# A spectrum stage interleaved with the next one, a half-group inverse over two PSUM buffers, and one DMA in place of four: a long convolution with gate and MLP on one core

## The chip, the cores and the metric

The kernel runs on one core of a Trainium2 chip. The metric is the device time of one execution in microseconds (us), as a median over several executions. Executions of one kernel agree within about 2%. Times from the profile ("span") are 1.7 to 2.2 us shorter than the device times.

In the views, PE, DVE, ACT, POOL and SP stand for TensorE, VectorE, ScalarE, GpSimd and SyncE, and PEld for TensorE's weight loads. An eviction is a copy out of PSUM, the memory into which matmuls write; a bank is here a piece of it of 128 x 512 f32, as in the views of evictions.

## The reference

```python
x  = A_q                                         # 2048 tokens x 512 channels
h  = x + A(_layernorm(x), k, v, shift_k, ssm_k, ssm_D)
h2 = h + relu(_layernorm(h) @ w1) @ w2           # 512 -> 1376 -> 512

def A(q, k, v, shift_k, ssm_k, ssm_D):
    kv = causal_4_tap(k, shift_k) * v
    y  = irfft(rfft(kv padded to 4096) * rfft(ssm_k padded to 4096))[:2048]
    return q * (y + kv * ssm_D)
```

The Fourier transforms are done as matmuls: 4096 = 64 x 64, so each transform is a "stage 1" and a "stage 2" with tables of sines between.

## The kernel before

The order on TensorE is: transposes and stage 1 of ssm_k (with the four taps of kv between), transposes of kv, spectrum of ssm_k (stage 2), stage 1 of kv, stage 2 of kv with the product, inverse stage 1, then groups of four token tiles through inverse stage 2, gate, layernorm and MLP. In the views, pst are the transposes, ps a stage 1, ps2k the spectrum of ssm_k, u and psy the product, psi and pz the two inverse stages, zt an evicted pz, st the statistics of a layernorm, pt and hlnT its transposed rows, ps1m and ps2m the two halves of the MLP. The parts that matter here (cut where dots stand):

```python
def _tokens(src2d, t0, nt):          # four patterns of 32 rows: token = 64 b + 16 a + t
    return [bass.AP(..., offset=... + (16 * a + t0) * D, ap=[[64 * D, 32], [1, nt * D]]) for a in range(4)]
...
def stage1(fl, a_out, engs, between=None):
    for gb in range(8):              # 64 small matmuls into 4 banks, then 4 evictions
        pss = [psum.tile([P, 8, 64], F32, tag="ps", ...) for r in range(4)]
        for gi in range(8):
            for f, first in ((f1hi, True), (f1lo, False)):
                for rg in range(4):  nc.tensor.matmul(out=pss[rg][:, gi, :], ...)
        for rg in range(4):  copy(engs[...], a_out[:, :, j0:j0 + 8], pss[rg]...)
...
for kp in range(16):                 # spectrum of ssm_k: 8 matmuls, an add on VectorE, a cast on ScalarE
    ...
stage1(xfl, a1x, "ADADADAA")         # then stage 1 of kv
...
for a, src in enumerate(_tokens(x_d, 0, NT)):     # x, 2 MB, after the product has freed the space
    nc.sync.dma_start(out=xh[32 * a:32 * a + 32, :, :]..., in_=src)
...
pzp = pl.push("psZ", bufs=1, space=PSUM)          # one buffer of 4 banks for the inverse
...
qln = ln1(0, on_act=True)
inv2_copy(0, inv2(0))
hln = new_rows(0)
gate(0, [0, 1], qln, hln, on_act=True)
gate(0, [2, 3], qln, hln, on_act=True)
pz = inv2(1)
transposes(0, hln)
mlp1(0, slice(0, 2 * P))
transposes(2, hln)
inv2_copy(1, pz)
mlp1(0, slice(2 * P, 4 * P))
chain(1)                             # layernorm, gate, layernorm, DMA transposes of group 1
inv2_copy(2, inv2(2))
mlp2(0)
chain(2)
...
```

## Time and profile before

| | before |
|---|---|
| time, median (3 fast runs) | 240.22 us (240.03 to 240.64) |
| span of the profile | 238.6 us |
| TensorE, VectorE, ScalarE busy | 206.1, 154.2, 130.7 us |

On the page, each digit of a strip is one fortieth of the span, about 6 us; PEclk is the clock that TensorE was granted, in tenths. The clock strip of the kernel before:

```profile
PEclk9999999999955899999999779999999999999998
```

There are two places of lowered clock: stage 1 of kv (65.6 to 79.3 us) and the stretch around the start of the MLP (two pieces of 3.41 us, from 133.9 and from 140.7). Before each of the two places TensorE was idle for a good part of the time: in the 3.41 us before, it was busy for 2.2 and for 1.2 us.

### The profile page before, as it was taken

To read this page: it belongs to the slowest core of one execution; us is meant where nothing else is said; L and a number is where in the kernel's file an instruction comes from. 1 tells how busy PE (TensorE), PEld (TensorE's weight loads), DVE (VectorE), ACT (ScalarE), POOL (GpSimd) and SP (SyncE) were. 2 spreads that over 40 slices of the span, in tenths; PEclk is the share of its full clock that TensorE was granted. 3 is DMA by queue.
4 is the path that set the end of the run, shared out by engine and by line. 5 is a ranking of instruction groups with operands and counts; after the bars stand their busy time and mean duration, and the time that the engine had idled before them with its cause. 6 is when DMAs were issued, how large, how long until landed. Compare 5 with 4: busy or idle time off the path is not lost.

```text
span 238.6 us, 7218 instructions
## 1 busy us (share of the span) xinstructions
PE 206.1 (86%) x3100; PEld 145.8 (61%) x3100; DVE 154.2 (65%) x299; ACT 130.7 (55%) x241; POOL 62.7 (26%) x88
## 2 busy tenths in 40 slices
PE   0486998999767999998989678899999999979992
PEld 0473555999646999978986546764446444434440
DVE  7886986877655989977995882822577257740031
ACT  3779464666775688897992338912262327105500
POOL 6399700000003999975000001020022002200000
PEclk9999999999955899999999779999999999999998
DMA  6999910000000000009992000023200420042011
GB/s 212 286 206 157 190 34 4 3 1 0 3 5 3 3 1 0 3 1 201 195 368 70 3 3 0 3 46 69 61 8 3 93 71 17 0 91 65 23 44 44
DMA packets 30191, 15.45 MB, mean 65 GB/s; under 512 B 25584, under 2 KB 29008, under 8 KB 30032
## 3 DMA queue, kind: packets, MB, share of 16 engines
q1 hardware_dynamic: 29088, 14.93, 28.3%
q8 instruction: 24, 0.39, 0.7%
q10 hardware_dynamic: 1072, 0.07, 0.4%
q14 instruction: 7, 0.06, 0.1%
HBM read 7.08 MB, written 2.10 MB: 38 GB/s over the span
## 4 chain that ended last, share of the span: by engine, by line
PE 79%; ACT 9%; DMA 5%; DVE 4%; issue 2%; SPq 0%; ACTq 0%
PE ps1m L486 16%; PE ps2m L496 15%; PE pz L417 9%; PE psi L389 6%; PE pst L196 5%; PE psy L326 5%; PE pkv L254 5%; PE u L226 4%; PE u L228 4%; DMA sk<-in_A_ssm_k_dram 4%; PE ps L212 3%; PE ps2k L226 3%; PE ps2k L228 3%; ACT zt L425 2%; ACT c2c L174 2%
## 5 line engine op out<-in xcount | busy, mean ns | idle before, releaser
L488 ACT ACTIVATE h1T<-ps1m 128x512 bf16<-128x512 f32 (+3 forms) x55 | 28.0, 515 | 39.3 <-PE ps1m L486 38.5
L486 PE MATMUL ps1m<-hlnT,w 128*128 128x512 bf16 (+3 forms) x220 | 40.5, 346 | 4.5 <-ACT hlnT L508 2.2
L496 PE MATMUL ps2m<-w,h1T 128*128 128x512 bf16 (+1 forms) x176 | 38.7, 379 | 0.0
L486 PEld LDWEIGHTS <-w 128*128 128x128 bf16 (+1 forms) x220 | 22.6, 103 | 22.1 <-issue 5.3
L499 DVE TENSOR_TENSOR o<-ps2m,xh 128x512 bf16<-128x512 f32 x16 | 11.0, 691 | 38.2 <-PE ps2m L496 38.2
L316 DVE TENSOR_TENSOR t<-u,kf 128x704 fp32r<-128x704 f32 x32 | 27.1, 889 | 4.8 <-ACT usb L312 4.8
L496 PEld LDWEIGHTS <-h1T 128*128 128x128 bf16 (+1 forms) x176 | 17.0, 98 | 21.1 <-issue 0.8
L316 POOL TENSOR_TENSOR t<-usb,kf 128x320 fp32r<-128x320 f32 x32 | 28.7, 924 | 3.4 <-ACT usb L312 2.3
L417 PE MATMUL pz<-bp,ecore 32*32 32x128 f32 x1024 | 22.1, 387 | 4.2 <-ACT zt L425 2.2
L434 POOL TENSOR_SCALAR rstd<-mv 128x4 f32<-128x4 f32 x6 | 1.4, 229 | 88.5 <-DVE mv L441 88.5
L417 PEld LDWEIGHTS pz<-bp,ecore 32*32 32x32 f32 x1024 | 15.8, 108 | 9.8 <-issue 2.9
L439 DVE BATCH_NORM_STATS2 st<-xh 128x6 f32<-128x512 bf16 x32 | 19.8, 680 | 0.0
L328 ACT CAST kf<-psy 128x512 fp32r<-128x512 f32 x32 | 18.4, 645 | 1.6
L389 PE MATMUL psi<-dre,kf 128*128 128x256 f32 x64 | 15.8, 288 | 0.9 <-ACT kf L328 0.9
L425 ACT CAST zt<-pz 128x512 bf16<-128x512 f32 x16 | 8.2, 602 | 13.9 <-PE pz L417 13.9
L326 PE MATMUL psy<-t,ipos 128*128 128x512 f32 x48 | 15.8, 390 | 0.0
L389 PE MATMUL psi<-dim,kf 128*128 128x256 f32 x64 | 15.4, 283 | 0.0
L254 PE MATMUL pkv<-kT,wdiag 128*128 128x512 bf16 x64 | 15.2, 381 | 0.0
L196 PE MATMUL pst<-ident,sk 128*128 128x128 bf16 x64 | 6.7, 299 | 9.2 <-DMA sk<-in_A_ssm_k_dram 9.2
L201 ACT CAST a1k<-ps 128x512 fp32r<-128x512 f32 x20 | 10.4, 593 | 6.7 <-PE ps L212 6.7
L283 DVE TENSOR_TENSOR kf<-ps2k,dtab 128x512 fp32r<-128x512 f32 x16 | 11.0, 694 | 3.5 <-PE ps2k L228 3.4
L284 ACT CAST kf<-ps2k 128x512 fp32r<-128x512 f32 x16 | 10.2, 641 | 5.5 <-PE ps2k L228 5.3
(108 smaller groups left out, 410.0 us busy)
## 6 DMA issues: line engine op xcount, KB each, us to landing
sk<-in_A_ssm_k_dram SPq DMA_DIRECT2D x1, 2048.0 KB, 8.4
xh<-in_A_q_dram SPq DMA_DIRECT2D x4, 512.0 KB, 8.6
out_dram<-o SPq DMA_DIRECT2D x64, 32.0 KB, 1.6
w<-in_B_w_dram SPq DMA_DIRECT2D x1, 1376.0 KB, 15.1
w<-in_B_w_dram SPq DMA_DIRECT2D x1, 1280.0 KB, 18.2
hlnT<-hln SPq DMA_TRANSPOSE x12, 2.5
w<-in_B_w_dram SPq DMA_DIRECT2D x1, 96.0 KB, 17.8
dtab<-in_A_ssm_D_dram ACTq DMA_DIRECT2D x2, 32.0 KB, 8.4
```

Source lines behind the costliest of these rows:

```text
L196: nc.tensor.transpose(out=pst[:, i, :], in_=src[:, :, :, 8 * q + i], identity=ident[:])
L226: nc.tensor.matmul(out=ps[:, kk, :], lhsT=w_re[:, k1, :], rhs=a_in[:, k1, :], start=True, stop=False, skip_group_check=True)
L254: nc.tensor.matmul(out=ps[:], lhsT=wdiag[:, rg, j, :], rhs=kT[c][:, rg, 16 - j:CH + 16 - j], start=(j == 0), stop=(j == KS - 1))
L316: eng.tensor_tensor(out=t[:, :, j, :], in0=in0.unsqueeze(1).to_broadcast([P, 2, n, 2]), in1=kfr[:, :, j, ks], op=ALU.mult)
L326: nc.tensor.matmul(out=psy[:], lhsT=m_[:], rhs=t_.rearrange("p j k -> p (j k)"), start=first, stop=not first)
L328: nc.scalar.copy(out=kf[:, s, :, 2 * kp:2 * kp + 2], in_=psy[:].rearrange("p (j k) -> p j k", k=2))
L389: nc.tensor.matmul(out=ps[:, i, :], lhsT=kf[:, c, 4 * m:4 * m + 4, :].rearrange("p r k -> p (r k)"), rhs=d[:].rearrange("p a b -> p (a b)" ...
L417: nc.tensor.matmul(out=pz[32 * a:32 * a + 32, r4, l4, :], lhsT=ecore[rows, rho, n2, :], rhs=rhs, start=(rho == 0), stop=(rho == 1), tile_p ...
L439: nc.vector.bn_stats(out=st[:, t % 4, :], in_=xh[:, t, :])
L486: nc.tensor.matmul(out=ps1[:fsz, :], lhsT=w1[:, c, fc * P:fc * P + fsz], rhs=hlnTs[sc][:, c, part], start=(c == 0), stop=(c == DC - 1))
L488: nc.scalar.activation(out=h1s[sc][:fsz, fc, part], in_=ps1[:fsz, :], func=ACT.Relu)
L496: nc.tensor.matmul(out=ps2[:], lhsT=h1s[sc][:ksz, fc, i * P:(i + 1) * P], rhs=w2[:ksz, fc, :], start=(fc == 0), stop=(fc == NFC - 1))
```

## The change

The change has five parts. (A) Half of the ssm_k spectrum runs alone, the other half between the first four groups of stage 1 of kv; kv's result overwrites the half of ssm_k's that is used up, so columns and tables are laid out by halves. (B) The inverse stage 2 of the first two groups goes in halves over two PSUM buffers of four banks. (C) The layernorm of the next group is issued ahead of mlp2. (D) The four patterns of 32 rows become one pattern of (4, 32) rows, for the load of x and for the output stores. (E) The small table dtab is loaded in four transfers instead of two. Cut to its core:

```diff
-    return [bass.AP(..., offset=src2d.offset + (16 * a + t0) * D, ap=[[64 * D, 32], [1, nt * D]])
-            for a in range(4)]
+    return bass.AP(..., offset=src2d.offset + t0 * D, ap=[[16 * D, 4], [64 * D, 32], [1, nt * D]])
...
-    for kp in range(16):
-        ... spectrum step kp ...
-    stage1(xfl, a1x, "ADADADAA")
+    for kp in range(8):
+        spectrum_k(kp)
+    for gb in range(8):
+        stage1(gb, xfl, lambda h, j: a1x[:, h, :, j:j + 8], "ADADADAA" if gb >= 4 else "ADAD")
+        if gb < 4:
+            spectrum_k(8 + 2 * gb)
+            spectrum_k(9 + 2 * gb)
...
-    for a, src in enumerate(_tokens(x_d, 0, NT)):
-        nc.sync.dma_start(out=xh[32 * a:32 * a + 32, :, :].rearrange("p t d -> p (t d)"), in_=src)
+    nc.sync.dma_start(out=xh[:].rearrange("p t d -> p (t d)"), in_=_tokens(x_d, 0, NT))
...
-            for a, dst in enumerate(_tokens(out_d, t, 1)):
-                nc.sync.dma_start(out=dst, in_=o[32 * a:32 * a + 32, :])
+            nc.sync.dma_start(out=_tokens(out_d, t, 1), in_=o[:])
...
-    inv2_copy(0, inv2(0))
     hln = new_rows(0)
-    gate(0, [0, 1], qln, hln, on_act=True)
-    gate(0, [2, 3], qln, hln, on_act=True)
-    pz = inv2(1)
+    for ts in ([0, 1], [2, 3]):
+        inv2_copy(0, ts)
+        gate(0, ts, qln, hln, on_act=True)
+    for ts in ([0, 1], [2, 3]):
+        inv2_copy(1, ts)
+    pl.pop("psZ0")                   # two buffers of 4 banks until here
+    ... push psT, psM, psZ ...
     transposes(0, hln)
-    mlp1(0, slice(0, 2 * P))
-    transposes(2, hln)
-    inv2_copy(1, pz)
+    mlp1(0, slice(0, 2 * P), lambda: transposes(2, hln))
     mlp1(0, slice(2 * P, 4 * P))
-    chain(1)
-    inv2_copy(2, inv2(2))
+    chain(1, ln1(1))
+    inv2_copy(2)
+    qln = ln1(2)
     mlp2(0)
-    chain(2)
+    chain(2, qln)
...
```

More of the change, by code (lines that the diff above doesn't have):

```diff
@@ L51, in _tokens @@
     D = src2d.shape[1]
-    return [bass.AP(tensor=src2d.tensor, offset=src2d.offset + (16 * a + t0) * D, ap=[[64 * D, 32], [1, nt * D]])
-            for a in range(4)]
+    return bass.AP(tensor=src2d.tensor, offset=src2d.offset + t0 * D, ap=[[16 * D, 4], [64 * D, 32], [1, nt * D]])
 @with_exitstack
@@ L97 @@
     nc.scalar.dma_start(out=wsh[:], in_=A_shift_k.rearrange("(r p) j -> p r j", p=P))
-    dtab = consts.tile([P, DC, 64], BF16, name="dtab")
+    dtab = consts.tile([P, 2, DC, 32], BF16, name="dtab")
     for dp in range(2):
-        src = bass.AP(tensor=A_ssm_D.tensor, offset=A_ssm_D.offset + 64 * dp, ap=[[0, 64], [P, DC], [1, 64]])
-        nc.scalar.dma_start(out=dtab[64 * dp:64 * dp + 64, :, :], in_=src)
+        for h in range(2):
+            src = bass.AP(tensor=A_ssm_D.tensor, offset=A_ssm_D.offset + 64 * dp + 32 * h,
+                          ap=[[0, 64], [P, DC], [1, 32]])
+            nc.scalar.dma_start(out=dtab[64 * dp:64 * dp + 64, h, :, :], in_=src)
     vT = vp.tile([P, DC, S], BF16, name="vT")
@@ L161 @@
     f1f = early.tile([P, 64], F32, name="f1_f")
-    _sin(f1f[:, 0:32], t1[:, 0:32], 128)
-    _sin(f1f[:, 32:64], t1[:, 32:64], 128, neg=True)
+    f1v = f1f[:].rearrange("p (h c k) -> p c h k", h=2, c=2)
+    _sin(f1v[:, 0], t1[:, 0:32].rearrange("p (h k) -> p h k", h=2), 128)
+    _sin(f1v[:, 1], t1[:, 32:64].rearrange("p (h k) -> p h k", h=2), 128, neg=True)
     cc = wp.tile([P, 32, P], F32R, name="c2c")
@@ L203, in copy, with stage1, col @@
             nc.vector.tensor_copy(out=o, in_=i)
-    def stage1(fl, a_out, engs, between=None):
-        for gb in range(8):
-            pss = [psum.tile([P, 8, 64], F32, tag="ps", name=f"ps1_{r}") for r in range(4)]
-            for gi in range(8):
-                for f, first in ((f1hi, True), (f1lo, False)):
-                    for rg in range(4):
-                        rows = slice(32 * rg, 32 * rg + 32)
-                        nc.tensor.matmul(out=pss[rg][:, gi, :],
-                                         lhsT=fl[rows, 8 * gb + gi, :, :].rearrange("p d n -> p (d n)"),
-                                         rhs=f[rows, :], start=first, stop=not first, tile_position=(32 * rg, 0))
-            for rg in range(4):
-                j0 = 64 * rg + 8 * gb
-                copy(engs[(4 * gb + rg) % len(engs)], a_out[:, :, j0:j0 + 8], pss[rg][:].rearrange("p g c -> p c g"))
-            if between is not None:
-                between(gb)
+    def stage1(gb, fl, a_out, engs):
+        pss = [psum.tile([P, 8, 64], F32, tag="ps", name=f"ps1_{r}") for r in range(4)]
+        for gi in range(8):
+            for f, first in ((f1hi, True), (f1lo, False)):
+                for rg in range(4):
+                    rows = slice(32 * rg, 32 * rg + 32)
+                    nc.tensor.matmul(out=pss[rg][:, gi, :],
+                                     lhsT=fl[rows, 8 * gb + gi, :, :].rearrange("p d n -> p (d n)"),
+                                     rhs=f[rows, :], start=first, stop=not first, tile_position=(32 * rg, 0))
+        for rg in range(4):
+            copy(engs[(4 * gb + rg) % len(engs)], a_out(gb // 4, 32 * rg + 8 * (gb % 4)),
+                 pss[rg][:].rearrange("p g c -> p c g"))
+    def col(k1, c):
+        return 32 * (k1 // 16) + 16 * c + k1 % 16
     def stage2(ps, a_in, kp, s):
@@ L225, in stage2 @@
             w_re, w_im = ((cc, cs), (cn, cc))[s]
-            nc.tensor.matmul(out=ps[:, kk, :], lhsT=w_re[:, k1, :], rhs=a_in[:, k1, :], start=True, stop=False,
+            nc.tensor.matmul(out=ps[:, kk, :], lhsT=w_re[:, k1, :], rhs=a_in(col(k1, 0)), start=True, stop=False,
                              skip_group_check=True)
-            nc.tensor.matmul(out=ps[:, kk, :], lhsT=w_im[:, k1, :], rhs=a_in[:, 32 + k1, :], start=False, stop=True,
+            nc.tensor.matmul(out=ps[:, kk, :], lhsT=w_im[:, k1, :], rhs=a_in(col(k1, 1)), start=False, stop=True,
                              skip_group_check=True)
@@ L246 @@
     nc.gpsimd.memset(dim[:].bitcast(F32), 0.0)
-    a1k = slotA.tile([P, 64, 256], F32R, tag="A", name="a1k")
+    a1 = slotA.tile([P, 64 * 256], F32R, tag="A", name="a1")
+    a1k = a1[:].rearrange("p (c j) -> p c j", j=256)
+    a1x = a1[:].rearrange("p (h c j) -> p h c j", h=2, j=P)
     def taps(u):
@@ L261, in two_taps @@
         taps(2 * gb + 1)
-    stage1(kfl, a1k, "ADAADADA", two_taps)
+    for gb in range(8):
+        stage1(gb, kfl, lambda h, j: a1k[:, :, P * h + j:P * h + j + 8], "ADAADADA")
+        two_taps(gb)
     for pq in halves:
@@ L276, with spectrum_k @@
     kf = slotB.tile([P, 2, 256, 32], F32R, tag="B", name="kf")
-    dcol = dtab[:].rearrange("p r g -> p (r g)").unsqueeze(2).to_broadcast([P, 256, 2])
-    for kp in range(16):
+    dcol = dtab[:].rearrange("p h r g -> p (h r g)").unsqueeze(2).to_broadcast([P, 256, 2])
+    def spectrum_k(kp):
         ks = slice(2 * kp, 2 * kp + 2)
@@ L281 @@
         for s in range(2):
-            stage2(ps[s], a1k, kp, s)
+            stage2(ps[s], lambda c: a1k[:, c, :], kp, s)
         nc.vector.tensor_tensor(out=kf[:, 0, :, ks], in0=ps[0][:].rearrange("p k j -> p j k"), in1=dcol, op=ALU.add)
         nc.scalar.copy(out=kf[:, 1, :, ks], in_=ps[1][:].rearrange("p k j -> p j k"))
-    a1x = slotA.tile([P, 64, 256], F32R, tag="A", name="a1x")
-    stage1(xfl, a1x, "ADADADAA")
+    for kp in range(8):
+        spectrum_k(kp)
+    for gb in range(8):
+        stage1(gb, xfl, lambda h, j: a1x[:, h, :, j:j + 8], "ADADADAA" if gb >= 4 else "ADAD")
+        if gb < 4:
+            spectrum_k(8 + 2 * gb)
+            spectrum_k(9 + 2 * gb)
     pl.pop("psF")
@@ L308, in product @@
             u = psum.tile([P, 2, 256], F32, tag=f"u{s}", name=f"u{s}")
-            stage2(u, a1x, kp, s)
+            stage2(u, lambda c: a1x[:, :, c, :], kp, s)
             usb = prod.tile([P, 256 - NJ, 2], F32, tag=f"usb{s}", name=f"usb{s}", bufs=2)
@@ L385 @@
         ps = psum.tile([P, 2, 2 * P], F32, tag="ps", name="psi1")
+        h, r, g = b // 16, b // 4 % 4, b % 4
+        m0 = 16 * r + 8 * h + 2 * g
         for i in range(2):
@@ L390 @@
                                  rhs=d[:].rearrange("p a b -> p (a b)"), start=(c == 0), stop=(c == 1))
-        copy("ADAADADA"[b % 8], bp[:, 2 * b:2 * b + 2, :, :, :].rearrange("p g a b c -> p g (a b c)"), ps[:])
+        copy("ADAADADA"[b % 8], bp[:, m0:m0 + 2, :, :, :].rearrange("p g a b c -> p g (a b c)"), ps[:])
         if b in (3, 10, 17):
@@ L398 @@
     pl.pop("psI")
-    pzp = pl.push("psZ", bufs=1, space=PSUM)
-    ptp = pl.push("psT", bufs=1, space=PSUM)
-    psum = pl.push("psM", bufs=3, space=PSUM)
+    pzp = pl.push("psZ0", bufs=2, space=PSUM)
     ep = pl.push("ep", bufs=2)
@@ L406, with inv2 @@
     zts, hlnTs, h1s = {}, {}, {}
-    def inv2(q):
+    def inv2(q, l4s=(0, 1, 2, 3)):
         pz = pzp.tile([P, 4, 4, P], F32, tag="pz", name="pz")
-        for l4 in range(4):
+        for l4 in l4s:
             for rho in range(2):
@@ L420, in inv2, with inv2_copy @@
         return pz
-    def inv2_copy(q, pz):
-        zts[q] = hp.tile([P, 4, D], BF16, tag="zt", name="zt")
-        for l4 in range(4):
+    def inv2_copy(q, l4s=(0, 1, 2, 3)):
+        pz = inv2(q, l4s)
+        if q not in zts:
+            zts[q] = hp.tile([P, 4, D], BF16, tag="zt", name="zt")
+        for l4 in l4s:
             nc.scalar.copy(out=zts[q][:, l4, :].rearrange("p (m r) -> p m r", r=4),
@@ L469, in new_rows, with chain @@
         return ep.tile([P, 4, D], BF16, tag="hln", name="hln")
-    def chain(q):
-        qln = ln1(q)
+    def chain(q, qln):
         hln = new_rows(q)
@@ L476, in chain, with mlp1 @@
             nc.sync.dma_start_transpose(out=hlnTs[q][:, :, i * P:(i + 1) * P], in_=hln[:, i, :])
-    def mlp1(sc, part=slice(0, 512)):
+    def mlp1(sc, part=slice(0, 512), midway=None):
         if sc not in h1s:
@@ L482, in mlp1 @@
         for fc in range(NFC):
+            if fc == NFC // 2 and midway is not None:
+                midway()
             fsz = min(P, DFF - fc * P)
@@ L510 @@
     qln = ln1(0, on_act=True)
-    inv2_copy(0, inv2(0))
     hln = new_rows(0)
-    gate(0, [0, 1], qln, hln, on_act=True)
-    gate(0, [2, 3], qln, hln, on_act=True)
-    pz = inv2(1)
+    for ts in ([0, 1], [2, 3]):
[4 more added lines that the diff above has]
+    pl.pop("psZ0")
+    ptp = pl.push("psT", bufs=1, space=PSUM)
+    psum = pl.push("psM", bufs=3, space=PSUM)
+    pzp = pl.push("psZ", bufs=1, space=PSUM)
     transposes(0, hln)
-    mlp1(0, slice(0, 2 * P))
-    transposes(2, hln)
-    inv2_copy(1, pz)
+    mlp1(0, slice(0, 2 * P), lambda: transposes(2, hln))
     mlp1(0, slice(2 * P, 4 * P))
-    chain(1)
-    inv2_copy(2, inv2(2))
+    chain(1, ln1(1))
+    inv2_copy(2)
+    qln = ln1(2)
     mlp2(0)
-    chain(2)
+    chain(2, qln)
     mlp1(1)
-    inv2_copy(3, inv2(3))
+    inv2_copy(3)
+    qln = ln1(3)
     mlp2(1)
-    chain(3)
+    chain(3, qln)
     for sc in (2, 3):
```

## The prediction

The sum came to 240.2 - 4.9 + 2.0 - 1.5 + 0.1 = 235.9 us with four engines for x, and to 229.8 with 16; the forecast between them was 235.0.

> **What bounds the kernel now.** I read the page's table of busy time first. TensorE is busy 206.1 of 238.6 us, but VectorE (154.2) and ScalarE (130.7) take turns in setting the pace, so an average says little. I then cut the span into stages by busy time of each engine in each stretch. Columns: stretch, its length, then busy us (and instructions) of PE, weight loads, DVE, ACT, POOL, then granted clock, DMA share, GB/s.
>
> ```profile
> core 0: us, PE busy (x) PEld busy (x) DVE busy (x) ACT busy (x) POOL busy (x), PEclk, DMA share, GB/s
> ...
> 45.60:61.10 15.50, 15.50 (x138) 15.37 (x140) 11.90 (x17) 10.09 (x16) 0.00 (x0) 1.00 0.01 2
> 61.10:74.80 13.70, 8.36 (x514) 6.67 (x513) 7.82 (x13) 10.77 (x21) 0.79 (x2) 0.67 0.02 5
> ```
>
> The first row is the ssm_k spectrum: TensorE is full, both evicting engines have a third free. The second is stage 1 of kv: 512 tiny matmuls, which TensorE could do in about 5 us (0.61 us for each of 8 groups), but 32 evictions of PSUM pace it and TensorE even drops to 0.67 clock. The timeline gives the cost of evictions:
>
> ```profile
> 46.89 2.00 DVE L283 TENSOR_TENSOR kf<-ps2k,dtab 128x512 fp32r<-128x512 f32 x3
> ...
> 61.83 2.54 ACT L201 CAST a1x<-ps 128x512 fp32r<-128x512 f32 x5
> 65.04 2.54 ACT L201 CAST a1x<-ps 128x512 fp32r<-128x512 f32 x5 [0.66 <-PE ps L212]
> ```
>
> So 0.51 us for an ACT eviction, 0.67 for a DVE spectrum add. After this, the product stage (to 105 us) is DVE's, and untouched. Then the chain of waits, for the inverse stage 2 (L417) and what follows:
>
> ```profile
> 131.31 2.06 ACT zt L425 x4
> 133.37 0.04 issue
> 133.42 4.58 PE pz L417 x188
> ...
> 140.02 1.02 ACT hlnT L508
> ...
> 148.00 1.01 ACT hlnT L508
> 149.01 1.96 ACT zt L425 x4
> ...
> 212.29 2.45 DMA hlnT<-hln
> ```
>
> TensorE stands still for 2.2 us while ACT empties the only pz buffer, 1.1 us twice for hlnT, 0.8 us because zt delays the ReLUs, and 1.5 us for the last DMA transpose. From 155 us TensorE is otherwise back to back. The last lines I need concern x, which the first layernorm reads:
>
> ```profile
> 107.25 1.74 SPq L344 DMA_DIRECT2D xh<-in_A_q_dram  x4
> ...
> xh<-in_A_q_dram SPq DMA_DIRECT2D x4, 512.0 KB, 8.6
> ...
> 124.19 2.46 DVE L439 BATCH_NORM_STATS2 st<-xh 128x6 f32<-128x512 bf16 x4
> ```
>
> x is issued at 107.25 and used at 124.19; DVE comes to it straight from the last bp copy, so the load has slack. Its slowest quarter lands 11.5 us after issue, near 119: some 5 us of slack.
>
> [...]
>
> **The change, part by part.** Times are on the clock of the profile of before.
>
> *A, spectrum beside stage 1.* The first 8 of 16 spectrum steps run alone: 8 x 0.96 = 7.7 us, to 53.3. Then four rounds of one stage-1 group and two spectrum steps. TensorE: 0.61 + 2 x 0.96 = 2.53 us. DVE: 2 x 0.63 + 2 x 0.67 = 2.59. ACT: 2 x 0.51 + 2 casts of 0.64 at most = 2.3. The round is even, 2.6 us, so four end at about 64.0 (first evictions at 54.05, TensorE's last work of them at 63.4, a little lag on DVE). The other four groups stand alone as before: in the trace two pairs of groups take 5.75 us from the first eviction (61.83) to the tenth ACT copy (65.04 + 2.54). End 64.0 + 5.8 = 69.8 against 74.7 now: -4.9 us, all on the path. The second half's eviction overwrites what the last spectrum step has read by then, so no new wait. I count nothing for the clock, which can still drop in the lone half.
>
> *B, half groups over two buffers, x on time.* ACT's order becomes root, zt half, root, zt half, ... Let X be the start of the x statistics. From the trace: statistics to normalised rows 4.8 us; gate of a half 4.3, its root after 3.0. Gate one X+4.8 to X+9.1; root ends X+8.1; zt of rows 2,3 to X+9.2; gate two ends X+13.4, its root X+12.4; zt of group 1's first half X+13.4 frees the banks for the transposes; its second half X+14.4; hlnT copy X+15.4; the MLP starts at X+15.5. With X = 124.2 that is 139.7 instead of 141.1. Then mlp1(0): 6.4 us in the half-clock start, 0.5 for the transposes now inside it, 5.1 for the second half without waits: it ends 12.2 us later, at 151.9 instead of 155.0: -3.0.
>
> *C, norms ahead of mlp2.* The last transposes come several us earlier (a 5.5 us norm leaves the path before gate 3): the 1.5 us wait at 213 goes. -1.5.
>
> *D, one DMA for four.* [...] 4 engines would carry 2 MB, 512 KB each. Estimate of one engine's rate: the DMA view of 100 to 130 us, in slices of 0.75 us, peaks at 407 GB/s over 16 while w1 and w2 load, 25.4 GB/s each:
>
> ```profile
> GB/s 0 0 0 0 0 0 0 11 0 0 66 284 284 131 240 218 153 306 131 240 262 131 284 58 183 283 385 407 385 355 352 354 347 348 302 71 48 0 0 0
> ```
>
> 524,288 B / 25.4 = 20.6 us; plus 1 us to the first byte, x lands near 129.2, and X moves from 124.2 to 129.2, +5.0 us, exposed in full because B's whole chain hangs on X. B then gives -3.0 + 5.0 = +2.0. The outputs, too, go over 4 engines: 32 rows of 1 KB each; at 48 ns a row (packet time in the trace) 1.5 us instead of 0.1. Three issues fewer (3 x 0.42 us) at the very end pay for it: +0.1. Over 16 engines it would be -1.0.
>
> *E.* dtab in 4 small transfers: 1.8 us more of issue on ACT, which idles 2.1 us there. 0.
>
> Sum with D [...]: 240.2 - 4.9 + 2.0 - 1.5 + 0.1 = 235.9. With 16 engines: 240.2 - 4.9 - 3.0 - 1.5 - 1.0 = 229.8.
>
> **Rivals.** R1: x is late (sum 235.9). For it: [...] that X leads the whole chain. Against: [...] the lowering might reorder the pattern. R2: x is in time (229.8). I give R1 three in four. R3: A gains less: the lone stage-1 groups wait for instructions (1 us issue gaps inside pairs in the chain), or interleaving makes DVE fall behind and hold banks; all 8 are used in a round. That would leave -3 of -4.9 and make R1 238. R4: TensorE, starved while x is awaited, sits at half clock longer into mlp1(0): +1 to +1.5 on R1, to 237. R5: eight small evictions more evenly spread keep the clock at 1.0 into the product: a further -0.4.
>
> **Range and chances.** The two sums are 6 apart. Weighted 3:1 they give 234.4; I take 235.0, near the likelier one. Range 229.5 to 238.0: R2 with a small bonus below, R1 with R3 above. The 2% line is 235.4. R2 lies below it nearly surely (0.24 of 0.25); of R1, its middle being 235.9 and its spread 1.5, about 0.4 lies below (0.30 of 0.75). That is 0.54; slower by 2% needs A to fail as well: 0.03.
>
> **What would show it.** A: the stretch from the last pst transposes to the first u takes 24.2 us, not 29.1. B: no ACT wait between the first two inverse groups other than on buffer two; no hlnT wait in mid mlp1(0). C: no DMA wait before the last mlp1. D decides: DVE's first wait on x. If the statistics wait on the x load for about 5 us, and its landing time is near 21 us, R1 holds; if x lands in under 16 us, R2. I am wrong altogether if A's stretch hardly shrinks or a new wait opens in the MLP.

The 1 us to the first byte is that of the kernel before: x is issued at 107.25 us and its first row starts at 108.24.

## The result

The changed kernel is slower: 260.06 us median (257.51 to 261.73, 4 runs) beside 240.43 us for the kernel before (4 runs, one of them, 243.92, slow). The ratio is 1.079 (95% interval 1.068 to 1.089). A ratio here is the mean time of one kernel's runs over that of the other's of the same rounds, so it is not quite the ratio of the medians. Executions over 1.5% slower than the fastest of the same kernel are left out of the means. The outputs are correct. The prediction said 235.0 us, range 229.5 to 238.0: wrong by 25 us, and on the wrong side.

The one profile of the changed kernel is of a run 1.6% above that kernel's fastest. Nothing below rests on that 1.6%, which is 4.2 us: the main wait is 24.6 us, and a wait of 23.3 us for the same load is found in a fast run (run 3).

The clock strip and the statistics row of the changed kernel's page show at once where to look. In the row: busy us, mean ns of one, then idle time before them and what ended it. Before:

```profile
L439 DVE BATCH_NORM_STATS2 st<-xh 128x6 f32<-128x512 bf16 x32 | 19.8, 680 | 0.0
```

Changed:

```profile
PEclk9997999999959999999965555599999999999998
...
L455 DVE BATCH_NORM_STATS2 st<-xh 128x6 f32<-128x512 bf16 x32 | 19.8, 679 | 24.6 <-DMA xh<-in_A_q_dram 24.6
```

VectorE stood still for 24.6 us for x, and TensorE ran at half clock from 131.6 to 169.2 us. The chain of waits of the changed kernel (start, length, what):

```profile
105.53 41.60 DMA xh<-in_A_q_dram
147.16 2.47 DVE st L455 x4
...
159.08 1.94 ACT zt L441 x4
161.07 1.02 PE pt L523 x8
162.17 1.02 ACT hlnT L524
163.23 4.42 PE ps1m L503 x20
```

The load of x takes 41.6 us from issue to landing, and the MLP cannot start before 163.2. Next, both kernels cut into the same six stretches: from the last transposes of kv to the first matmul of the product, to the first inverse matmul of stage 2, to the MLP's first matmul, to the inverse of group 2, to the last matmul, to the end. The first, the third and the fourth line carry the reading (columns as in the prediction). Before:

```profile
45.71:74.73 29.02, 23.68 (x640) 21.86 (x639) 19.71 (x29) 20.75 (x37) 0.79 (x2) 0.84 0.01 3
...
124.99:141.08 16.09, 12.16 (x520) 8.80 (x521) 11.80 (x36) 5.20 (x9) 0.00 (x0) 0.88 0.11 33
141.08:154.97 13.89, 12.01 (x107) 9.93 (x114) 8.48 (x23) 10.72 (x26) 1.28 (x2) 0.89 0.00 1
```

Changed:

```profile
47.84:73.43 25.59, 22.18 (x641) 20.69 (x639) 20.33 (x31) 20.21 (x35) 0.79 (x2) 0.94 0.01 4
...
123.28:163.23 39.95, 12.37 (x520) 9.25 (x521) 14.28 (x43) 7.00 (x13) 0.35 (x2) 0.60 0.21 56
163.23:176.33 13.10, 13.10 (x107) 10.69 (x114) 10.65 (x32) 8.95 (x22) 2.20 (x3) 0.77 0.07 13
```

The whole account, with the lengths of the other stretches:

| stretch | before | changed | difference |
|---|---|---|---|
| start to the end of kv's transposes | 45.71 | 47.84 | +2.1 |
| spectrum and stage 1 of kv | 29.02 | 25.59 | -3.4 |
| product, inverse stage 1 | 50.26 | 49.85 | -0.4 |
| inverse stage 2 to the MLP's start | 16.09 | 39.95 | +23.9 |
| first mlp1 | 13.89 | 13.10 | -0.8 |
| to the last matmul | 79.08 | 77.80 | -1.3 |
| to the end | 4.55 | 5.47 | +0.9 |
| span | 238.6 | 259.6 | +21.0 |

So the stretches of A and C and the first mlp1 are shorter, in sign as forecast, and one stretch eats it all.

### The profile page after: what moved, and what is told of

The parts are those of the page before. It is cut to its first block, busy times and chain, and to the rows that moved or that the text cites. A ratio compares the mean times of both kernels' runs of the same rounds, so it can differ in the third digit from the quotient of the medians.

```text
span 259.6 us, 7149 instructions
## 1 busy us (share of the span) xinstructions
PE 205.9 (79%) x3085; PEld 146.0 (56%) x3100; DVE 154.4 (59%) x301; ACT 130.2 (50%) x239; POOL 62.2 (24%) x88
## 4 chain that ended last, share of the span: by engine, by line
PE 66%; DMA 19%; DVE 6%; ACT 5%; issue 2%; POOLq 0%; DVEq 0%; ACTq 0%
DMA xh<-in_A_q_dram 16%; PE ps1m L503 16%; PE ps2m L513 15%; PE psy L341 6%; PE pst L198 5%; PE pkv L261 5%; PE pz L431 4%; DMA sk<-in_A_ssm_k_dram 3%; PE u L229 3%; PE ps2k L229 3%; PE u L231 3%; PE ps L214 3%; PE ps2k L231 3%; DVE st L455 2%; ACT c2c L176 2%
## 5 line engine op out<-in xcount | busy, mean ns | idle before, releaser
L503 PE MATMUL ps1m<-hlnT,w 128*128 128x512 bf16 (+3 forms) x217 | 41.3, 352 | 1.3 <-ACT hlnT L524 1.2
L455 DVE BATCH_NORM_STATS2 st<-xh 128x6 f32<-128x512 bf16 x32 | 19.8, 679 | 24.6 <-DMA xh<-in_A_q_dram 24.6
L203 ACT CAST a<-ps 128x512 fp32r<-128x512 f32 x38 | 19.9, 594 | 9.4 <-PE ps L214 9.2
L205 DVE CAST a<-ps 128x512 fp32r<-128x512 f32 x26 | 16.8, 686 | 5.8 <-PE ps L214 5.7
L447 ACT ACTIVATE rstd<-mv,eps_t 128x2 f32<-128x2 f32 (+1 forms) x3 | 0.9, 297 | 31.8 <-DVE mv L457 31.8
L261 PE MATMUL pkv<-kT,wdiag 128*128 128x512 bf16 x56 | 15.9, 402 | 0.6 <-issue 0.2
```

The source lines that it names most:

```text
L203: nc.scalar.copy(out=o, in_=i)
L261: nc.tensor.matmul(out=ps[:], lhsT=wdiag[:, rg, j, :], rhs=kT[c][:, rg, 16 - j:CH + 16 - j], start=(j == 0), stop=(j == KS - 1))
L455: nc.vector.bn_stats(out=st[:, t % 4, :], in_=xh[:, t, :])
L503: nc.tensor.matmul(out=ps1[:fsz, :], lhsT=w1[:, c, fc * P:fc * P + fsz], rhs=hlnTs[sc][:, c, part], start=(c == 0), stop=(c == DC - 1))
```

## The experiments

The theory after reading the traces: D alone makes the loss; the x load runs on four engines (in the trace 116 of its 128 rows of 16 KB start with four under way; in the kernel before it is 16 to 18 for 111 of 128), and those slow one another down. The rivals: the interleaving or the half-group order is itself harmful; or the engines do not slow one another down.

**1. The changed kernel with x in four transfers again.**

```diff
-    nc.sync.dma_start(out=xh[:].rearrange("p t d -> p (t d)"), in_=_tokens(x_d, 0, NT))
+    for a, src in enumerate(_tokens4(x_d, 0, NT)):
+        nc.sync.dma_start(out=xh[32 * a:32 * a + 32, :, :].rearrange("p t d -> p (t d)"), in_=src)
```

> The changed kernel with one thing undone: x is loaded in four transfers of 32 rows again (outputs still in one transfer each). Theory D (the x load on four engines, [...] is nearly the whole loss): x lands 11 to 12 us after its issue, before VectorE is free for the statistics, no DMA wait there; time 234 to 237 us, against 240.2 before and about 260 changed. Rival I (the interleaved stage or the half-group inverse is itself the loss): the time stays at 245 us or above though x lands in time.

Measured 236.78 us (235.67 to 237.44), ratio to before 0.985 (0.978 to 0.991). One statement is worth 23 us. The statistics no longer wait for x. The interleaving and the half groups are not the loss.

**2. The same with the output stores in four as well.**

> The changed kernel with both the x load and the output stores in four transfers again. Theory D: as the run with only the x load undone, less 0.5 to 1 us at the end, because the last store lands sooner [...] (233 to 236 us). Rival (one store per tile is cheaper, three issues of 0.42 us saved): this run is up to 1 us slower than the run with only the x load undone.

Measured 235.92 us (234.13 to 236.38), ratio 0.980 (0.974 to 0.987). That is 0.9 us under the first run, as the theory said, though the intervals overlap. This kernel has everything of the change but D, so the stretches of A, B and C are best read from it. From the same cuts as above, those of the spectrum with stage 1 of kv, of the first mlp1, and of the rest to the last matmul (its stretch from the first inverse matmul to the MLP, 16.02 us, is in the chain further down):

```profile
46.54:71.65 25.11, 21.77 (x641) 20.36 (x639) 20.32 (x31) 20.17 (x35) 0.79 (x2) 0.99 0.02 4
...
137.23:150.22 12.99, 12.99 (x107) 10.76 (x113) 10.77 (x32) 8.85 (x22) 1.81 (x5) 0.78 0.16 21
150.22:227.44 77.22, 76.69 (x813) 37.77 (x820) 29.25 (x71) 24.17 (x42) 4.68 (x7) 1.00 0.21 43
```

**3. The kernel before with x in a single transfer, nothing else.**

> The kernel before with one thing added: x in a single transfer over (4, 32) rows. Theory D: landing about 41 us after issue instead of at most 11.5, VectorE's first statistics wait 24 to 25 us for it, time 263 to 267 us: slower than the changed kernel, which gains a few us elsewhere. Rival I: the load costs only a few us (under 246), the rest of the loss comes from the other parts of the change.

Measured 260.37 us (260.12 to 261.22), ratio 1.084 (1.077 to 1.091). The loss alone, without the rest of the change. I had expected 263 to 267, so this missed by 3 us, and its chain shows why:

```profile
107.26 40.28 DMA xh<-in_A_q_dram
147.56 2.47 DVE st L444 x4
...
160.59 6.63 PE ps1m L491 x44
```

From the statistics to the MLP it takes 13.0 us here, but 16.1 us in the changed kernel (147.16 to 163.23). When x is late, the old order runs all of group 1's inverse (152.6 to 158.9) while VectorE works on the gates. In the new one the last evictions of the inverse stand in ScalarE's queue behind the root of the second gate (158.79), and the transposes follow them at 161.07. B costs about 3 us in that state, by one profile of each. So the late x explains all of the loss, and B a part of what A and C could have given back.

**4. The kernel before with each output tile in one store.**

> The kernel before with one thing added: each output tile in one transfer over (4, 32) rows. Theory: 32 rows of 1 KB go one after another on each of four engines; the tail after the last output add grows from 3.8 to about 4.7 us, time 241.0 us (+0.3 to +1.2). Rival (issue cost rules): three issues fewer at the end, 239.2 us (-1).

Measured 240.85 us, ratio 1.002 (0.996 to 1.008): too small to tell in the time. In the profile the end after the last matmul is 5.0 us (233.62 to 238.6) against 4.55. The three saved issues do not pay for the four engines, but by little (in the changed kernel's trace, which has the same stores, the 128 rows of the last one take 1.76 us, mostly in fours that start 0.04 us apart, at 0.046 us a row; in the kernel before up to 14 rows of stores are under way at once).

**5 and 6. Why 41 us and not 21?** In the kernel before, the view of DMA from 109 to 118 us shows x's four transfers at work; each of them has 32 rows, and mostly 16 to 18 rows are under way at once:

```profile
DMA packets 166, 1.83 MB, mean 203 GB/s; under 512 B 51, under 2 KB 51, under 8 KB 55
```

203 GB/s over 16 engines is 12.7 GB/s for one, half of the 25.4 that I had estimated. In the changed kernel's trace x starts as four rows of 16 KB at once, at 107.77 to 107.80 us; these four take 0.61 us each, and most rows after them 1.2 to 1.3. By the one pattern of (4, 32) rows, the four begin at partitions 0, 32, 64 and 96 and step in parallel. Theory P of the next two runs is that it matters which rows are loaded side by side: that rows 0 to 31 beside 32 to 63, and 64 to 95 beside 96 to 127, hold each other up, and rows 32 to 63 beside 64 to 95 do not. (All these pairs are 32 partitions apart; where a text says "32 apart" for those that hold each other up, it means on one side of row 64.) Two kernels test this, each with two engines that carry most or all of x:

```diff
-    nc.sync.dma_start(out=xh[:].rearrange("p t d -> p (t d)"), in_=_tokens(x_d, 0, NT))
+    for p0, p1 in ((32, 96), (0, 32), (96, 128)):       # 6: ((0, 64), (64, 128))
+        src = bass.AP(..., offset=x_d.offset + 16 * (p0 // 32) * D,
+                      ap=[[16 * D, (p1 - p0) // 32], [64 * D, 32], [1, NT * D]])
+        nc.sync.dma_start(out=xh[p0:p1, :, :].rearrange("p t d -> p (t d)"), in_=src)
```

> The changed kernel with x in three transfers: first rows 32 to 95 over (2, 32) rows, so on two engines [...], then the outer two blocks of 32 rows on 16 engines each. Theory P [...]: an engine [...] moves a 16 KB row in about 0.63 us, 32 rows in about 20 us, so x lands about 21 to 25 us after issue, time about 242 to 245 us. Rival (an engine moves such rows at 13 GB/s whatever its neighbour does): 40 us or more to land, time 260 us as in the changed kernel.

> The changed kernel with x in two transfers over (2, 32) rows, rows 0 to 63 and then 64 to 127: again two engines only, as in the run with rows 32 to 95, but now the two (rows 0 to 31 beside 32 to 63, then 64 to 95 beside 96 to 127) step through partitions 32 apart. Theory P [...]: a row takes 1.25 us to the end, after w1 and w2 have landed too, 64 rows on each engine, x lands about 80 us after issue, time about 298 us. Rival (the rate fell because four engines were at work, or because of w1 and w2 alone): 0.61 us a row once w1 and w2 are in, as for rows 32 to 95; x lands after about 50 us, time about 270 us.

Measured: 252.93 us for run 5, rows 32 to 63 beside 64 to 95 (one run; x landed 33.0 us after its first issue), 284.28 us for run 6, rows 0 to 31 beside 32 to 63 and then 64 to 95 beside 96 to 127 (one run; VectorE waited 48.6 us). Neither number was expected: the first is between the theory's 25 us and the rival's 40, the second between 80 and 50. The rate while nothing else was moving is the cleaner reading. Run 5, 126 to 137 us, then run 6, 127 to 160 us:

```profile
DMA packets 40, 0.61 MB, mean 55 GB/s; under 512 B 3, under 2 KB 3, under 8 KB 3
```

```profile
DMA packets 71, 1.13 MB, mean 34 GB/s; under 512 B 2, under 2 KB 2, under 8 KB 2
```

Two engines move 27 GB/s each in run 5 (a row of 16 KB in 0.61 us), 17 each in run 6. In DRAM the two blocks of rows lie 16 KB apart in both kernels (the offset 16 * D), so the layout there does not tell them apart. By single rows of 16 KB in the trace: in run 5 most rows took 1.0 to 1.5 us until about 125 us, while w1 and w2 were landing, and 0.61 us from then on. In run 6, w1 and w2 but for a last 96 KB were in by 116 us, and nearly all packets from 127 to 160 us are rows of x; yet rows of 1.2 us go on to 162 us, mixed more and more with rows of 0.61. So it does matter which rows are loaded side by side, and the wrong ones double the time of a row (1.22 beside 0.61 us) where it bites; why is not shown, nor why the first four rows of the changed kernel took only 0.61. That the traffic of w1 and w2 does the same, and that the mixture comes from two engines drifting apart in their steps, fits the rows but is not tested by itself. My 80 us had taken the lockstep as permanent, my 25 us had forgotten w1 and w2. In the changed kernel, 512 KB in the 38.8 us from the first row to the last in the trace are 13.5 GB/s for one of four engines, the rate of rows of 1.2 us.

**7. Only A.** Inverse stage 2, order of norms, x and stores as before.

> Only the interleaving of the spectrum with stage 1 of kv (with its dtab layout and a1 views); x load, stores, inverse stage 2 and the order of norms as before. Theory: the stretch from the last transposes of xfl to the first u takes 26 us instead of 29, and the product starts no colder: 236.5 us (-3 to -4). Rival: the interleaving only moves the wait to the lone second half, and the time stays within 1 us of 240.

Measured 237.41 us (236.17 to 238.74), ratio 0.987 (0.978 to 0.996). The stretch takes 25.4 us (46.33 to 71.74). The rival, that the wait only moves and the time stays within 1 us of 240, falls.

**8. Only B and C.**

> Only the half-group inverse over two buffers and the norms ahead of mlp2; everything else as before. Theory I (TensorE runs short of instructions in the run of small matmuls, 0.8 us before each half, as the run with both transfers undone shows; the 2.2 us wait for the buffer is largely replaced): the MLP starts within 0.5 us of where it did (16 us after the first inverse matmul), gain 1 us in mlp1 and 1.5 us at the last transposes: 237.3 to 238.5 us. Rival (my prediction's step B holds): 235.7 us (-4.5).

Measured 240.31 us (239.36 to 242.19), ratio 1.000 (0.993 to 1.008). No gain that shows. My step B does not hold, and even the 2 us that theory I left did not come out in the time. In its profile the first inverse matmul is 1.5 us later than before, in part because a half-clock window fell on the taps (clock 0.79 from 22 to 30 us, 1.00 before), and from it to the last matmul it takes 106.55 us against 109.06. So in this one profile 2.5 us are there, and a lower clock likely took much of it. Whether that is chance is open: all four runs of this kernel had a lower mean clock (0.935 to 0.949) than the seven of the kernel before beside them (0.952 to 0.961).

**Where B's gain went** is seen in the chain of run 2, where x is in time:

```profile
121.21 4.42 PE pz L439 x186
125.64 0.22 issue
125.86 2.75 PE pz L439 x116
128.61 0.81 issue
129.42 2.76 PE pz L439 x114
132.18 0.81 issue
132.99 1.33 PE pz L439 x45
134.34 1.08 ACT zt L449 x2
...
137.23 4.43 PE ps1m L511 x20
```

The 2.2 us wait for the buffer (before, 131.2 to 133.4) is gone, but TensorE now waits 1.84 us for nothing that the profile shows, in three "issue" gaps. The MLP starts 16.0 us after the first inverse matmul, as before (16.1). The same gaps of about 1 us (0.95, 1.05 and 0.85) stood in stage 1 of kv before the change. A half of an inverse group is 128 matmuls with 128 weight loads. In stage 1 before, the view of DMA from 60 to 75 us has four packets on a queue that it calls "instruction", and nothing else:

```profile
DMA packets 4, 0.07 MB, mean 4 GB/s; under 512 B 0, under 2 KB 0, under 8 KB 0
...
q8 instruction: 4, 0.07, 1.7%
```

Four packets of 16 KB for 512 matmuls and their 512 loads, one for each pair of groups. The times of these packets in the traces say more than their number. In stage 1 before, packets end at 63.21, 66.56 and 70.03 us, and the issue gaps of the chain end at 64.54, 67.99 and 71.44. In run 2, packets end at 124.56, 127.98 and 131.71, and the gaps end at 125.86, 129.42 and 132.99. All six gaps end 1.28 to 1.44 us after such a packet, as if TensorE had waited for it. The same holds, within 1.2 to 1.6 us, for 59 of the 60 gaps of 0.12 us or more between matmuls in the chains of all fourteen profiles (for 8 of 9 in those of before and changed; there the ninth ends 2.07 us after). That they carry TensorE's instructions is read from the queue's name and these times.

**9. The kernel before with the low half of the table left out in stage 1 of kv** (less exact).

```diff
-    stage1(xfl, a1x, "ADADADAA")
+    stage1(xfl, a1x, "ADADADAA", both=False)      # 256 matmuls, not 512; the same 32 evictions
```

> The kernel before with the low half of the table left out in stage 1 of kv: 256 instead of 512 small matmuls, the same 32 evictions (the result is slightly wrong on purpose). Theory I (TensorE runs short of instructions in runs of small matmuls: pairs of groups, 256 instructions with their weight loads, came 3.45 us apart): the issue gaps of 0.9 to 1.0 us go, pairs come 2.5 to 2.7 us apart as ACT's five copies allow, the first u starts 2.3 us earlier. Rival (evictions, banks or the cold clock pace it): pairs stay 3.4 us apart.

Measured 236.97 us (one run). ScalarE's 20 evictions now come without a pause:

```profile
62.43 9.90 ACT L201 CAST a1x<-ps 128x512 fp32r<-128x512 f32 x20
```

Before, they took from 61.83 to 74.69, 12.9 us, in four blocks of 2.54 with gaps. Half the instructions, and the gaps are gone, though TensorE's own work was far below the evictions' all along. A cold clock as the cause is ruled out: it was at half for 13.65 us in both kernels, from 65.6 us before and from 64.7 here. With the packets' times this speaks for the supply of instructions as what paced this stage; the matmuls' own time fell with their number too, but it was never what the evictions waited for at full clock (0.61 us a group).

**10 and 11. Other orders of the inverse halves and the MLP**, x and stores in four. Run 10: halves 0a, 0b, 1a, then transposes and the first half of mlp1, then 1b. Run 11: only group 0 in halves, the first half of mlp1, then all of group 1.

> The changed kernel with x load and stores in four, and another order: inverse halves 0a, 0b, 1a over the two buffers, then the transposes of the first rows, the second gate after them, first half of mlp1, and only then the inverse half 1b. The MLP no longer waits for zt of 1b (it ended at 135.4, while the rows were ready at 129.3). Theory: MLP starts 11 us after the first inverse matmul instead of 16, TensorE idles 3 us less: 232.5 to 233.5 us. Rival: the cold clock and the instruction shortage move into mlp1, gain under 1 us (235 to 236).

> The changed kernel with x and stores in four and yet another order: only the two inverse halves of group 0 over the two buffers, then the first transposes, the second gate, the first half of mlp1, then all of the inverse of group 1, then the second half of mlp1. The small matmuls no longer come 1024 instructions in a row: mlp1's long matmuls stand between. Theory I: no issue gap over 0.5 us in group 1's inverse, MLP starts 8.5 to 9 us after the first inverse matmul (16 in the kernel before), the next inverse (of group 2) 25 us after it instead of 29: 231 to 233 us. Rival: time within 1 us of the run with both transfers undone (236).

Measured 236.13 us (ratio 0.982, 0.975 to 0.988) and 236.01 us (0.983, 0.978 to 0.988). Both rivals won. In run 10 the MLP starts 13.7 us after the first inverse matmul, not 11, with issue gaps of 0.85 and 1.08 us before it. In run 11 the MLP starts 9.85 us after the first inverse matmul, six sooner than in run 2, and still the inverse of group 2 comes 30.1 us after it (29.0 in run 2):

```profile
131.26 4.42 PE ps1m L511 x20
135.68 0.85 PE pt L532 x8
...
145.44 2.05 ACT zt L449 x4
147.49 0.30 ACT h1T L513
147.83 3.65 PE ps1m L511 x32
```

Its first 20 matmuls of mlp1 take 0.22 us each, at half clock (0.11 later), and the eviction of group 1 now holds the ReLUs up, as it did before the change. The idle time moved; it did not go.

**12. Run 2 again, five rounds.**

> The run with both transfers undone once more, in five rounds, because three left open whether it is 2% faster. Theory: 235.5 to 236.3 us, ratio 0.979 to 0.985, with stretches as in the first time: 16 us from the first inverse matmul to the MLP, no DMA wait of VectorE for x. Rival (the first time was a lucky set of clock windows): 237 us or more.

Measured 235.33 us (234.56 to 236.98), ratio 0.975 (0.970 to 0.980); the kernel before had 242.2 us in this set, somewhat slower than elsewhere. So the change without D is about 2 to 2.5% faster than the kernel before, and 9% faster than the changed kernel. It has the lowest median here, but runs 10 and 11 are not told apart from it (0.982 and 0.983 beside 0.980 and 0.975, on three chips). Its gain over the kernel before beyond run 7's (0.987) is not told apart from noise either.

## Why the prediction was wrong

The prediction named x's load as the point that decides (D, and R1), and it came out so: four rows of x are under way at once, all of the chain hangs on it. The step that failed is the estimate of the rate in D: "524,288 B / 25.4 = 20.6 us". With 1 us to the first byte (2.2 us in the changed kernel, 105.53 to 107.77) it stood for 21.6 us; x measured 41.6 us from issue to landing (40.3 in run 3). So VectorE waited 24.6 us for x and not 5.0 (X itself moved from 124.19 to 147.16, although x was issued 1.7 us sooner). That one term is nearly 20 of the 25 us by which the forecast missed. The 25.4 GB/s were taken from w1 and w2, which cover all 128 partitions. The transfer in question was in the same trace at half that rate, and it was x itself: 201 and 195 GB/s in the page's slices, which I read as the bandwidth of 16 engines and did not divide by 16. The weights 3:1 for R1 and R2 then put the range between two sums that were both wrong.

- **A** (-4.9): right in kind, -3.4 in the changed kernel, -3.6 alone, -3.9 in run 2. In the changed kernel four rounds took 10.9 us, not 10.7 (stage-1 groups at 55.57, 58.29, 61.01, 63.73 and 66.45 in the chain). The sum counted the lone second half from its first eviction and so left out 0.7 us of matmuls before it (66.45 to 67.16). The half itself took 6.2 us, not 5.8, with an issue gap of 1.3 us instead of 0.95. No step saw a new wait, as said.
- **B** (-3.0): the order of ScalarE's queue was right, the MLP came at X+16.1 for a forecast X+15.5. But with x in time it gave about -1.0: nothing at the MLP's start, 0.9 in mlp1. Two things were missed. TensorE stood in issue gaps between the halves (three, 1.84 us in all, in run 2; that it ran short of instructions there is read from the packets of run 2 and from run 9; R3 had this for stage 1 only), and the transposes waited for the last eviction of the inverse (161.02 before 161.07), not for the first half's, so the freed banks helped nobody.
- **C** (-1.5): -1.3 in the changed kernel, -1.9 in run 2. The wait for the last DMA transposes is gone. Right.
- **D at the end** (+0.1): +0.9 in the changed kernel, +0.4 in run 4. Right in sign; the times do not resolve it.
- **E** (0): the load of ssm_k landed 0.6 us later in the changed kernel, 0.2 in run 2. The remaining 1.5 of the +2.1 in the first stretch go with a half-clock window on the taps. It hit run 8 too (clock 0.79 from 22 to 30 us), whose early part is that of before (1.00), and run 1 but not run 2 (0.79 and 1.00), which are the same up to the output stores; so it comes and goes without a change of the program. One thing lies outside the span: device time less span is 2.1 to 2.2 us in the kernels with A and its four table loads and 1.7 to 1.9 in the others. Why was not looked for.
- **R4** (cold start of mlp1): real, clock 0.77 in the first mlp1 with x late; but 0.78 in run 2 as well.
- **The clock**, on which R4 rests: in the kernel before, half-clock stretches began at 65.63 and 133.90 us, after 3.41 us in which TensorE was busy for 2.20 and 1.21 us, with no pause longer than 0.95 and 2.20 us. Whether idleness brings them on, and how much of it, is not shown.

## What to carry to other kernels

Before merging DMAs, look at the outermost dimension of the merged pattern (here 32 rows outermost went 16 to 18 at once, 4 outermost four at once) and at the partitions that will be written in the same moment (27 GB/s for an engine in run 5, 17 in run 6); here three issues fewer for each store did not show in the time, and one load on 4 of 16 engines cost 23 us. Take the rate for a transfer from the same transfer in the trace, not from the fastest one. And where a run of small matmuls has a wait in it, ask what else goes on during that wait before counting its removal as a gain.
